# Half of the last 64 rows of wq read through GpSimd's queue, on one core of Trainium2: a decode step with a long key and value cache

## The chip, the cores and the metric

The kernel runs on one core of a Trainium2 chip. Its engines are TensorE (PE in the profile; PEld is its weight load), VectorE (DVE), ScalarE (ACT), GpSimd (POOL) and SyncE (SP). The metric is the time of one execution in device microseconds (us); lower is better. Comparisons below are of medians of several runs, and a profile is of one execution.

A DMA is issued by an engine's instruction and is carried out by the core's 16 DMA engines. In the profile the DMAs issued by SP are queue q1, those issued by ACT are q10, and q8 and q14 are fetches of instructions. "SPq", "ACTq" and "DVEq" stand for those engines' own sequencers. The trace also has a record for every DMA packet: its start, its duration, its size and its queue (which DMA engine carried it is not in the record).

## The reference

```python
def reference(A_x, A_k_cache, A_v_cache, A_wq, A_wo, B_x, B_w1, B_b1, B_w2, B_b2, gate_w):
    x = A_x                                        # (1, 1, 448), bf16
    g = _sigmoid((x * gate_w).sum(-1, keepdims=True))
    # a: 16 query heads over 8 key/value heads, 65536 cached positions, 256 per head
    q = (x @ wq).reshape(B, Sq, Hq, Dh).transpose(0, 2, 1, 3)
    scores = einsum("bhqd,bhkd->bhqk", q, repeat(k_cache, 2)) * Dh ** -0.5
    a = einsum("bhqk,bhkd->bhqd", softmax(scores), repeat(v_cache, 2)) ... @ wo
    # b: layernorm(x), then a small MLP over the sequence axis of length 1, 1792 wide
    b = gelu(layernorm(x) * w1 + b1) @ w2 + b2
    return g * a + (1 - g) * b
```

The two caches are 268 MB each; wq is 448 x 4096 (3.7 MB) and wo 4096 x 448 (3.7 MB). Everything else is small.

## The kernel before, in words

**Blocks.** The 65536 positions of each of the 8 key/value heads are cut into 4 blocks of 16384, so there are 32 blocks (L = 31 is the last). A block of keys or of values is 128 partitions x 64 KB, 8 MB, and is read by one DMA from SP's queue. Keys go to three half-block slots of `k_all`, values to `vt`. For each block DVE transposes keys (L395, eight times 128x2048), PE makes scores from them (L403, 64 matmuls), a running softmax follows (L460 to L504), and PE multiplies the probabilities with the values (L423). A loop (L581) runs 15 times over two blocks; the last two blocks are written out behind it (L615 to L680), where the values of block 31 come in eight pieces, the last two of 4 positions per partition each, and where wo's last piece is the last load.

**The head of the kernel.** Before the loop the kernel makes the queries and the small MLP. SP issues, in this order: the first 384 rows of wq (`wq_m`, L157: 128 partitions x 24 KB), the last 64 rows (`wq_t`, L158: each row in two halves, so that row r's halves are partitions 2r and 2r+1 with 4 KB each), then three loads of the keys of block 0 (L124: two of 2 MB and one of 4 MB). Both wq tiles lie in `vt`, so that the first load of values (L133) must wait until the queries are made. ACT issues x (`xr`), then the three small tables w1, b1 and w2 (L166; 14 rows of 256 bytes each, into `tables`), then `gw` and `b2b`.

POOL writes a constant (`ident`, by a memset and an affine select) and sets `qz` to zero (L206). DVE makes masks from `ident` (L176 to L188). Among them is `par`, which says to which of the two halves a partition of `wq_t` belongs. L217 doubles each of the last 64 values of x into `xrr`, in the order of the partitions of `wq_t`; a matmul turns it into a column (L226), and L234 multiplies it with `par` into `xtm`, the weights for `wq_t`.

The tables are transposed on PE (L248) and then read by DVE (L258, L259); DVE finishes the layernorm (L260 to L268), and ACT makes 14 gelu tiles (L273). PE makes the queries: for each of 32 columns three matmuls with `wq_m` (L284) and one with `wq_t` (L291). They are copied and spread by L299 to L317 (into `qz`). Then come memsets (L376 to L380), the gate's sum (L331, L332), ACT's `ez` (L333), and DVE's end of the MLP (L342 to L353), while PE sums the gelu tiles (L337). Then the loop is entered; all engines meet there, and SP issues the first load of values (L133).

**The order.** Each engine's instructions stand in the order of the program text (the helper `seq` ties each instruction to the one before it on its engine). The framework adds the waits; a DMA's completion semaphore is one of eight per kind of queue in turn, so that SP's second load of the head that takes a semaphore used before waits for the DMA that had it (L124's second load waits for `wq_m`).

Of the kernel before, what the change touches and what calls it, by code (L numbers as in the profile page):

```python
# [9 lines left out]
BF16 = mybir.dt.bfloat16  # L10
ACT = mybir.ActivationFunctionType
ALU = mybir.AluOpType
AXIS = mybir.AxisListType
# [4 lines left out]
REP = HQ // HKV  # L18
# [13 lines left out]
def kernel(  # L32
# [15 lines left out]
    nc = tc.nc  # L48

    D = A_x.shape[-1]  # L50
# [3 lines left out]
    NF = F // 128  # L54
# [6 lines left out]
    def seq(ins):  # L61
        e = ins.ins.engine
        if e in last:
            tc.add_manual_dep(
                ins.ins,
                last[e],
                mybir.DependencyInfo(
                    mybir.DependencyClass.NoSync, mybir.DependencyReason.DATA
                ),
                reason="program order",  # L70
            )
        last[e] = ins.ins.name
        return ins

    kvpool = ctx.enter_context(tc.tile_pool(name="kvpool", bufs=1))
    const = ctx.enter_context(tc.tile_pool(name="const", bufs=1))
# [24 lines left out]
    xr = const.tile([1, D], BF16)  # L101
    gw = const.tile([1, D], BF16)
    tables = const.tile([3 * NF, 128], BF16)
    w2b = const.tile([128, NF], BF16)
    b2b = const.tile([1, 1], BF16)
    DM = 384
    wq_m = vt[:, 0:48, :].rearrange("p a b -> p (a b)").rearrange("p (k n) -> p k n", k=3)
    wq_t = vt[:, 48:56, :].rearrange("p a b -> p (a b)")
# [40 lines left out]
    def load_v_last(n):  # L149
# [5 lines left out]

    seq(nc.scalar.dma_start(out=xr[:], in_=A_x[0, 0].rearrange("(o n) -> o n", o=1)))
    seq(nc.sync.dma_start(out=wq_m, in_=A_wq[0:DM, :].rearrange("(p k) n -> p k n", k=3)))  # L157
    seq(nc.sync.dma_start(  # L158
        out=wq_t[:, :], in_=A_wq[DM:D, :].rearrange("r (h n) -> (r h) n", h=2)
    ))  # L160
    for k, table in enumerate((
        B_w1[0].rearrange("(b p) -> b p", p=128),
        B_b1.rearrange("(b p) -> b p", p=128),
        B_w2.rearrange("(b p) o -> b (p o)", p=128),
    )):
        seq(nc.scalar.dma_start(out=tables[k * NF:(k + 1) * NF, :], in_=table))  # L166
    seq(nc.scalar.dma_start(out=gw[:], in_=gate_w.rearrange("(o n) -> o n", o=1)))
    seq(nc.scalar.dma_start(out=b2b[:], in_=B_b2.rearrange("(o n) -> o n", o=1)))
    load_k(0, 1, 1, ((0, 32), (32, KP)))
# [2 lines left out]

    ident = const.tile([128, 128], BF16)
    make_identity(nc, ident[:])
    ident_f = const.tile([128, 128], FP32)
    seq(nc.vector.tensor_copy(out=ident_f[:], in_=ident[:]))  # L176
    rowsel = ident_f[:].rearrange("p (a i r) -> p r a i", a=4, r=REP)
# [2 lines left out]
        out=val[:], in_=rowsel[:, :, :, 0:NI], op=ALU.add, axis=AXIS.XY  # L180
    ))
    fst = const.tile([128, 2, REP], FP32)
    for e in range(2):
        seq(nc.vector.tensor_reduce(
            out=fst[:, e, :], in_=rowsel[:, :, :, e:e + 1], op=ALU.add, axis=AXIS.XY
        ))
    par = const.tile([128, REP], FP32)
    seq(nc.vector.tensor_reduce(  # L188
        out=par[:], in_=ident_f[:].rearrange("p (a r) -> p r a", r=REP), op=ALU.add, axis=AXIS.X
    ))  # L190
    nval = const.tile([128, REP], FP32)
    seq(nc.vector.tensor_scalar(
        out=nval[:], in0=val[:], scalar1=-scale, scalar2=None, op0=ALU.mult
# [7 lines left out]
        out=same[:], in_=val[:].unsqueeze(1).to_broadcast([128, 64, REP])  # L201
# [7 lines left out]
        out=sel[:],  # L209
        in_=ident[:].rearrange("p (w k) -> p w k", w=NW).unsqueeze(2).to_broadcast([128, NW, NQ, 32]),  # L210
# [2 lines left out]

    xm = const.tile([128, 3], BF16)
    xtm = const.tile([128, REP], BF16)
    xrr = const.tile([1, D - DM, 2], BF16)
    seq(nc.vector.tensor_copy(  # L217
        out=xrr[:], in_=xr[:, DM:D].unsqueeze(2).to_broadcast([1, D - DM, 2])
    ))
    x_col = hd_ps[:, 40:44]  # L220
    for k in range(3):
        seq(nc.tensor.matmul(
# [1 line left out]
            rhs=ones_b[:, 0:1], start=True, stop=True,  # L224
        ))
    seq(nc.tensor.matmul(  # L226
        x_col[:, 3:4], lhsT=xrr[:].rearrange("o a r -> o (a r)"),
        rhs=ones_b[:, 0:1], start=True, stop=True,
    ))
    seq(nc.tensor.matmul(  # L230
# [4 lines left out]
        out=xtm[:], in0=par[:], scalar1=x_col[:, 3:4], scalar2=None, op0=ALU.mult  # L235
# [13 lines left out]
        t_ps, lhsT=tables[:, :], rhs=ident[0:3 * NF, 0:3 * NF], start=True, stop=True  # L249
# [5 lines left out]
        out=veps[:], in0=mv[:, 1:2], scalar1=1e-5, scalar2=None, op0=ALU.add  # L255
# [5 lines left out]
    for _ in range(2):  # L261
# [3 lines left out]
            out=ntmp[:], in0=ntmp[:], scalar1=-0.5, scalar2=1.5, op0=ALU.mult, op1=ALU.add  # L265
# [3 lines left out]
        out=h_bc, in0=xf, scalar1=mv[:, 0:1], scalar2=rstd[:, 0:1],  # L269
        op0=ALU.subtract, op1=ALU.mult,  # L270
    ))
    for b in range(NF):
        seq(nc.scalar.activation(  # L273
            out=gel[b], in_=h_bc, func=ACT.Gelu_apprx_tanh,
# [4 lines left out]
    for h in range(HQ):  # L279
        half, hh = divmod(h, HQ // 2)  # L280
        for c in range(2):
            col = c * HQ + h
            for k in range(3):
                seq(nc.tensor.matmul(  # L284
                    q_ps[:, col:col + 1],
                    lhsT=wq_m[:, k, h * DH:(h + 1) * DH].rearrange("p (d c) -> p c d", c=2)[:, c, :],
# [6 lines left out]
                lhsT=wq_t[:, hh * DH:(hh + 1) * DH].rearrange("p (d c) -> p c d", c=2)[:, c, :],  # L293
# [7 lines left out]
    for w in range(NW):  # L301
        seq(nc.tensor.matmul(
            qq_ps[:, w * 2 * HQ:(w + 1) * 2 * HQ],
            lhsT=sel[:, w, :, :].rearrange("p a k -> p (a k)"), rhs=qb[:],
# [3 lines left out]
    for k in range(2):  # L308
        seq(nc.vector.tensor_copy(
            out=qq[:, :, :, k, :], in_=qq_ps.rearrange("p (w g r) -> p w g r", g=HKV, r=REP)  # L310
# [304 lines left out]
    for n in (L - 1, L):  # L615
# [14 lines left out]
        else:  # L630
            def rest_base():
# [9 lines left out]
                out=lsv[:], in0=val[:], scalar1=lsum[:, 0:1], scalar2=None, op0=ALU.mult  # L641
# [8 lines left out]
                out=rdv[:], in0=rdv[:], scalar1=gcol[:, 0:1], scalar2=None, op0=ALU.mult  # L650
# [6 lines left out]
    for c in range(2):  # L657
        for e in range(2):
            seq(nc.tensor.matmul(
                o_last[:, c, :],  # L660
                lhsT=acc[:, e, :].rearrange("p (d c) -> p c d", c=2)[:, c, :],
# [5 lines left out]
        out=oT[:], in0=o_last, in1=rdv[:].unsqueeze(1).to_broadcast([128, 2, REP]), op=ALU.mult  # L667
# [43 lines left out]
```

## Time and profile before

| what | value |
|---|---|
| median of 3 runs | 1265.22 us (1265.11 to 1265.61) |
| the profiled execution's own time | 1265.1 us |
| its span in the profile | 1263.3 us |
| HBM read | 544.22 MB, 431 GB/s over the span |
| busy: PE, DVE, ACT, POOL | 805.5, 708.2, 59.5, 1.7 us |
| DMA packets | 13494 |

The span runs from the first instruction shown to the last; 1.8 us of the execution's own time lie outside it. Busy times say how long an engine worked, not what the kernel waits for. The DMA row of the profile gives, for 40 equal slices of the span, the mean busy share of the 16 DMA engines in tenths.

### The profile page before, as it was taken

The page shows a single profiled execution, that of the slowest core. Times are in us where ns is not written, and L with a number is a line of the kernel's source. Part 1 is how long each engine was busy: PE and PEld are TensorE (multiplying, and loading weights), DVE is VectorE, ACT ScalarE, POOL GpSimd, SP SyncE. Part 2 cuts the span into 40 slices and gives each one's busy share as a digit, 9 for nine tenths or more (in the row PEclk, how much of TensorE's full clock was granted, in tenths as well). Part 3 has the DMA queues.
Part 4 walks back from the last instruction along what each step waited for, and adds up shares of the span by engine and source line. Part 5 has one row for each costly group of instructions (what it writes and reads, how often), then busy time and mean ns, then how long its engine had stood idle before and what let it go on. Part 6 is the DMA issues. An engine that isn't in the chain of part 4 may idle for free.

```text
span 1263.3 us, 12073 instructions
## 1 busy us (share of the span) xinstructions
PE 805.5 (64%) x4690; PEld 319.1 (25%) x4690; DVE 708.2 (56%) x755; ACT 59.5 (5%) x132; POOL 1.7 (0%) x7
## 2 busy tenths in 40 slices
PE   4756567575576656666566766658666576665568
PEld 2222222222222222222222222213222232222224
DVE  4665456664556645566444665446654456654575
ACT  4000000000000000000000000000000000000000
POOL 0000000000000000000000000000000000000000
PEclk9977788777888777878778887788877787877879
DMA  9999999999999999999999999999999999999998
GB/s 414 430 439 432 433 438 432 433 438 433 432 438 433 432 435 436 426 440 436 429 438 422 442 438 422 442 424 438 440 424 436 435 432 436 435 432 439 427 437 343
DMA packets 13494, 544.36 MB, mean 431 GB/s; under 512 B 1577, under 2 KB 3628, under 8 KB 4140
## 3 DMA queue, kind: packets, MB, share of 16 engines
q1 hardware_dynamic: 13394, 544.22, 99.6%
q8 instruction: 6, 0.10, 0.0%
q10 hardware_dynamic: 90, 0.01, 0.0%
q14 instruction: 4, 0.03, 0.0%
HBM read 544.22 MB, written 0.00 MB: 431 GB/s over the span
## 4 chain that ended last, share of the span: by engine, by line
DMA 71%; PE 12%; DVE 12%; issue 4%; SPq 0%; DVEq 0%
DMA k_all<-in_A_k_cache_dram 67%; DVE kT L395 12%; PE sc L403 11%; DMA vt<-in_A_v_cache_dram 2%; DMA k_all<-in_A_v_cache_dram 2%; PE hd_ps L539 0%; SPq L130 0%; PE hd_ps L525 0%; PE f L672 0%; PE sm_ps L525 0%; DVEq L395 0%; DVE res L678 0%; PE hd_ps L448 0%; SPq L124 0%; DVE oT L666 0%
## 5 line engine op out<-in xcount | busy, mean ns | idle before, releaser
L403 PE MATMUL sc<-kT,qz 128*128 128x512 bf16 x2048 | 545.1, 416 | 322.1 <-DVE kT L395 321.8
L395 DVE STREAM_TRANSPOSE kT<-k_all 128x2048 f32<-128x2048 f32 x256 | 570.7, 2282 | 210.2 <-DMA k_all<-in_A_k_cache_dram 160.2
L403 PEld LDWEIGHTS <-qz 128*128 128x128 bf16 x2048 | 211.3, 103 | 658.2 <-issue 478.8
L423 PE MATMUL pv_ps<-vt,pT 128*4 128x512 bf16 x1968 | 175.2, 534 | 27.2 <-DVE pT L498 27.2
L504 DVE SCALAR_TENSOR_TENSOR acc<-acc,al,pv_ps 128x512 f32<-128x512 f32 x31 | 23.2, 747 | 163.6 <-PE pv_ps L423 163.6
L423 PEld LDWEIGHTS <-pT 128*4 128x4 bf16 x2000 | 58.0, 110 | 131.9 <-issue 88.0
L491 ACT ACTIVATE p_sb<-sc,nb 128x512 bf16<-128x512 f32 x32 | 22.0, 687 | 1031.5 <-DVE nb L487 1031.5
L460 DVE TENSOR_REDUCE rmax<-sc 128x1 f32<-128x512 f32 x32 | 22.1, 692 | 63.6 <-PE sc L403 63.6
L498 DVE STREAM_TRANSPOSE pT<-p_sb 128x512 bf16<-128x512 bf16 x32 | 22.8, 711 | 27.4 <-ACT p_sb L491 27.4
L510 PE MATMUL hd_ps<-lsum,same 128*128 128x1 f32 x30 | 7.6, 322 | 28.8 <-DVE lsum L499 28.8
L478 PE MATMUL sm_ps<-mrun,ones_f 1*128 1x2 f32 x64 | 12.1, 257 | 21.2 <-DVE mrun L477 13.0
L464 PE MATMUL sm_ps<-ident_f,rmax 128*1 128x128 f32 x32 | 8.7, 270 | 24.5 <-DVE rmax L460 24.5
L546 ACT COPY wo_sb<-wo_sb 128x896 bf16<-128x896 bf16 x16 | 15.0, 937 | 149.5 <-PE hd_ps L539 142.3
L525 PE MATMUL hd_ps<-esc,acc 128*128 128x2 f32 x60 | 9.9, 269 | 17.2 <-DVE acc L504 13.1
L539 PE MATMUL hd_ps<-wo_sb,oT 128*1 128x448 bf16 x60 | 20.8, 452 | 0.0
L543 DVE TENSOR_TENSOR a_acc<-a_acc,hd_ps 1x448 f32<-1x448 f32 x15 | 9.1, 608 | 17.4 <-PE hd_ps L539 17.4
L478 PEld LDWEIGHTS sm_ps<-mrun,ones_f 1*128 1x128 f32 x64 | 9.4, 183 | 27.4 <-DVE mrun L477 16.3
L525 PEld LDWEIGHTS hd_ps<-esc,acc 128*128 128x128 f32 x60 | 8.6, 204 | 25.4 <-DVE acc L504 20.2
L510 PEld LDWEIGHTS hd_ps<-lsum,same 128*128 128x128 f32 x30 | 6.3, 261 | 30.1 <-DVE lsum L499 30.1
L487 DVE CUSTOM_DVE_ANT_0 junk<-sm_ps,nval 128x2 f32<-128x2 f32 x32 | 5.1, 160 | 14.0 <-PE sm_ps L478 14.0
L464 PEld LDWEIGHTS sm_ps<-ident_f,rmax 128*1 128x1 f32 x32 | 2.5, 80 | 40.1 <-DVE rmax L460 40.1
L317 DVE COPY qz<-qq 32x16 bf16 (+1 forms) x64 | 10.5, 164 | 1.4
(117 smaller groups left out, 149.1 us busy)
## 6 DMA issues: line engine op xcount, KB each, us to landing
k_all<-in_A_k_cache_dram SPq DMA_DIRECT2D x3, 4096.0 KB
vt<-in_A_v_cache_dram SPq DMA_DIRECT2D x1, 5120.0 KB, 27.3
k_all<-in_A_k_cache_dram SPq DMA_DIRECT2D x2, 2048.0 KB
k_all<-in_A_v_cache_dram SPq DMA_DIRECT2D x2, 2048.0 KB
wo_sb<-in_A_wo_dram SPq DMA_DIRECT2D x16, 224.0 KB, 27.9
vt<-in_A_wq_dram SPq DMA_DIRECT2D x1, 3072.0 KB
vt<-in_A_v_cache_dram SPq DMA_DIRECT2D x1, 3072.0 KB
k_all<-in_A_v_cache_dram SPq DMA_DIRECT2D x3, 1024.0 KB
```

The costliest lines, as they stand in the source:

```text
L395: seq(nc.vector.transpose(out=kT_tiles[i % 2][:].rearrange("p j w k c -> p (j w k c)").bitcast(FP32), in_=slots[pair[i // 4]][:, i % 4 * N ...
L403: seq(nc.tensor.matmul(sc_tiles[e][:, :], lhsT=qz[:, 2 * w + c, 2 * (NI - i):2 * (NI - i) + 128], rhs=kT_tiles[i % 2][:, :, w, :, c], star ...
L423: seq(nc.tensor.matmul(dst[32 * grp:32 * grp + 2 * REP, :, :], lhsT=pT[:, 32 * jj + 2 * REP * ip:32 * jj + 2 * REP * (ip + 1)], rhs=pairs( ...
L460: seq(nc.vector.tensor_reduce(out=rmax[:], in_=sc_ps[:, :], op=ALU.max, axis=AXIS.X))
L478: seq(nc.tensor.matmul(sm_ps[:, 128:128 + REP], lhsT=ones_f[0:1, :], rhs=mrun[0:1, :], start=True, stop=True))
L491: seq(nc.scalar.activation(out=p_sb[:, :], in_=sc_ps[:, :], func=ACT.Exp, scale=scale, bias=nb[:, 0:1], accum_out=den[:, 0:1],))
L498: seq(nc.vector.transpose(out=pT[:, :], in_=p_sb[:, :]))
L504: seq(nc.vector.scalar_tensor_tensor(out=acc[:], in0=acc[:], scalar=al_tiles[e][:, 0:1], in1=src[:, :, :], op0=ALU.mult, op1=ALU.add,))
L510: seq(nc.tensor.matmul(hd_ps[:, 460:461], lhsT=same[:].rearrange("p a r -> p (a r)"), rhs=lsum[:, 0:1], start=True, stop=True,))
L525: seq(nc.tensor.matmul(o_ps[c], lhsT=acc[:, e, :].rearrange("p (d c) -> p c d", c=2)[:, c, :], rhs=weights[:, e, :], start=(start and e == ...
L539: seq(nc.tensor.matmul(a_ps, lhsT=oT[:, c, r:r + 1], rhs=wo_sb[:, r, c, :], start=(r == 0 and c == 0), stop=(r == REP - 1 and c == 1),))
L546: seq(nc.scalar.copy(out=wo_sb[:, 0], in_=wo_sb[:, 1]))
```

## The change

Four things are changed, all ahead of the loop. The 64 rows are now laid out by halves: partition r of `wq_t` in 64 to 127 holds the second half of row r, and partitions 0 to 63 hold first halves. The second halves stay on SP's queue (64 rows of 4 KB). The first halves are read by a DMA that POOL issues, whose source has 8 as its outermost dimension: row 8s + a goes to partition 8a + s. Ahead of it POOL issues a DMA of the first 8 rows of w1; ACT issues only rows 8 to 13 of it. DVE builds `xrr` with two copies in the place of one, in the new order of the rows, and `par` sums over the two halves of the partitions.

```diff
--- before.py
+++ after.py
@@ -155,15 +155,15 @@
 
     seq(nc.scalar.dma_start(out=xr[:], in_=A_x[0, 0].rearrange("(o n) -> o n", o=1)))
     seq(nc.sync.dma_start(out=wq_m, in_=A_wq[0:DM, :].rearrange("(p k) n -> p k n", k=3)))
-    seq(nc.sync.dma_start(
-        out=wq_t[:, :], in_=A_wq[DM:D, :].rearrange("r (h n) -> (r h) n", h=2)
-    ))
+    halves = A_wq[DM:D, :].rearrange("r (h n) -> h r n", h=2)
+    seq(nc.sync.dma_start(out=wq_t[64:128, :], in_=halves[1]))
+    w1_rows = B_w1[0].rearrange("(b p) -> b p", p=128)
+    seq(nc.scalar.dma_start(out=tables[8:NF, :], in_=w1_rows[8:NF, :]))
     for k, table in enumerate((
-        B_w1[0].rearrange("(b p) -> b p", p=128),
         B_b1.rearrange("(b p) -> b p", p=128),
         B_w2.rearrange("(b p) o -> b (p o)", p=128),
     )):
-        seq(nc.scalar.dma_start(out=tables[k * NF:(k + 1) * NF, :], in_=table))
+        seq(nc.scalar.dma_start(out=tables[(k + 1) * NF:(k + 2) * NF, :], in_=table))
     seq(nc.scalar.dma_start(out=gw[:], in_=gate_w.rearrange("(o n) -> o n", o=1)))
     seq(nc.scalar.dma_start(out=b2b[:], in_=B_b2.rearrange("(o n) -> o n", o=1)))
     load_k(0, 1, 1, ((0, 32), (32, KP)))
@@ -172,6 +172,10 @@
 
     ident = const.tile([128, 128], BF16)
     make_identity(nc, ident[:])
+    seq(nc.gpsimd.dma_start(out=tables[0:8, :], in_=w1_rows[0:8, :]))
+    seq(nc.gpsimd.dma_start(
+        out=wq_t[0:64, :], in_=halves[0].rearrange("(s a) n -> a s n", a=8)
+    ))
     ident_f = const.tile([128, 128], FP32)
     seq(nc.vector.tensor_copy(out=ident_f[:], in_=ident[:]))
     rowsel = ident_f[:].rearrange("p (a i r) -> p r a i", a=4, r=REP)
@@ -186,7 +190,7 @@
         ))
     par = const.tile([128, REP], FP32)
     seq(nc.vector.tensor_reduce(
-        out=par[:], in_=ident_f[:].rearrange("p (a r) -> p r a", r=REP), op=ALU.add, axis=AXIS.X
+        out=par[:], in_=ident_f[:].rearrange("p (h r) -> p h r", h=2), op=ALU.add, axis=AXIS.X
     ))
     nval = const.tile([128, REP], FP32)
     seq(nc.vector.tensor_scalar(
@@ -213,10 +217,12 @@
 
     xm = const.tile([128, 3], BF16)
     xtm = const.tile([128, REP], BF16)
-    xrr = const.tile([1, D - DM, 2], BF16)
+    xrr = const.tile([1, 2, D - DM], BF16)
     seq(nc.vector.tensor_copy(
-        out=xrr[:], in_=xr[:, DM:D].unsqueeze(2).to_broadcast([1, D - DM, 2])
-    ))
+        out=xrr[:, 0, :].rearrange("o (a s) -> o a s", a=8),
+        in_=xr[:, DM:D].rearrange("o (s a) -> o a s", a=8),
+    ))
+    seq(nc.vector.tensor_copy(out=xrr[:, 1, :], in_=xr[:, DM:D]))
     x_col = hd_ps[:, 40:44]
     for k in range(3):
         seq(nc.tensor.matmul(
@@ -224,7 +230,7 @@
             rhs=ones_b[:, 0:1], start=True, stop=True,
         ))
     seq(nc.tensor.matmul(
-        x_col[:, 3:4], lhsT=xrr[:].rearrange("o a r -> o (a r)"),
+        x_col[:, 3:4], lhsT=xrr[:].rearrange("o h r -> o (h r)"),
         rhs=ones_b[:, 0:1], start=True, stop=True,
     ))
     seq(nc.tensor.matmul(
```

On POOL the order before was: memset of `ident`, memset of `qz`, affine select. It is now: memset of `ident`, the DMA of 8 table rows, affine select, the DMA of 64 half rows, memset of `qz`. The matmul L248 now waits for one more DMA (the 8 table rows), the first matmul with `wq_t` (L291 before) for both halves' DMAs, and the loop's first load of values for both too. All lines behind the change move down by 4 to 6.

## The prediction

> **What bounds the kernel now.** I read the page's DMA rows first, then the timeline and the waits of both ends, then the trace's packet records.
>
> ```profile
> span 1263.3 us, 12073 instructions
> PE 805.5 (64%) x4690; PEld 319.1 (25%) x4690; DVE 708.2 (56%) x755; ACT 59.5 (5%) x132; POOL 1.7 (0%) x7
> ...
> DMA  9999999999999999999999999999999999999998
> ...
> q1 hardware_dynamic: 13394, 544.22, 99.6%
> q8 instruction: 6, 0.10, 0.0%
> ```
>
> No compute engine is above 64% while the DMA engines are at 9 in all slices but the last: the kernel streams 544.22 MB, and a stage's compute matters only if it leaves them without work. The packet records are sharper. From 2.0 to 1257 us all 16 engines always have a packet in hand; a 64-KB packet starts 2.414 us after the one before it on its engine, so the records link into 16 chains, one for each engine. They are equal in bytes and unequal in time. At the last piece of values the earliest chain is done at 1257.0, most by 1258.2, and one, which I call the slow engine, at 1258.81. It got behind by 0.3 us with its first packet (2.03 us, where the row for 24 KB is 0.912) and by 1.4 us when a 16-KB instruction packet (q8) fell on it at 50.7. Other late ones at that point: 1258.23 and 1258.11 (a q8 packet each, at 1215 and 1248) and 1258.16.
>
> Two chains lead to the end, both through the slow engine. These are the timeline's rows (start, duration, engine, line, work, idle before and its releaser):
>
> ```profile
> 1200.92 4.50 DVE L395 STREAM_TRANSPOSE kT<-k_all 128x2048 f32<-128x2048 f32 x2 [6.34 <-DMA k_all<-in_A_k_cache_dram]
> ...
> 1259.20 0.35 PE L448 MATMUL hd_ps<-pT,k_all 128*128 128x2 bf16 x8 [0.16 <-DMA k_all<-in_A_v_cache_dram]
> ```
>
> DVE starts on block 30's keys after waiting 6.34 us for them: the slow engine's share ended at 1200.46, the next one's at 1199.53. From there DVE and PE run nearly without a gap, and at the end PE waits 0.16 us for the last values, again the slow engine's. Both move one for one with the slow engine; if only one moves, the other stops the gain after 0.16 us, or at once.
>
> So a change in the head counts in one of two ways: it empties the DMA queues, or it shifts work among the 16 engines. The rows for the first, the head's timeline:
>
> ```profile
> 11.78 0.19 DVE L258 COPY wb<-hd_ps 128x28 f32<-128x28 f32 x1 [4.44 <-PE hd_ps L248]
> ...
> 23.49 1.28 ACT L333 ACT_TABLE_LOAD   x1
> ...
> 25.02 0.14 DVE L342 TENSOR_SCALAR gate<-ez 1x1 f32<-1x1 f32 x1 [4.04 <-ACT ez L333]
> ...
> 28.09 0.35 SPq L133 DMA_DIRECT2D vt<-in_A_v_cache_dram  x1
> ```
>
> DVE idles 4.44 us for the tables and 4.04 us for ACT. The first load of values is issued at 28.09; from issue to first packet the first load took 1.03 us (0.74 to 1.77), so it is ready at 29.1, while the engines end block 0's keys between 30.37 and 31.37. That is a cover of 1.3 us, and of 2.0 us or more for the late engines.
>
> **The change part by part.**
>
> Bytes: none added or removed. At 431 GB/s nothing is won by the split as such.
>
> The spread over engines. In the trace a table of 14 rows puts one 256-byte packet on each of 14 chains and none on two, 128 rows put eight packets on each of 16, one row goes to one. Rows are dealt out by the outermost dimension. So 8 outermost should mean eight engines with eight rows each, and SP's 64 rows sixteen with four each. A 4-KB packet takes 0.159 us, 0.155 from start to start. Before, each engine had 8; after, eight engines have 12 and eight have 4. That is +0.62 us on one half of the engines and -0.62 on the other, and since no engine idles afterwards, it stays to the end. The 8 + 6 table rows move 18-ns packets, 0.04 us at most.
>
> [...] No row here shows a GpSimd DMA.
>
> Is the slow engine on the relieved half? The records have no engine numbers. The table rows ahead take eight engines first; if engines are dealt in turn, the half rows get the other eight, so I take the relieved half to be the low one (a choice, no row shows it) and rank the chains by their first packet: the engine that alone has `xr` and `gw` (number 0) is second at 1.790, the two without tables (14, 15) are 11th and 13th. The slow engine is third, at 1.792, so it is probably low. The late chains at 1258.16 (fourth) and 1258.11 (ninth) are low and doubtful; the one at 1258.23 started late (2.627) and can't be placed. With the slow engine relieved it ends at 1258.19. If a late chain is on the loaded half, it ends at 1258.73 to 1258.85 and becomes the new last: the gain is then between 0.08 and nothing. If none is, it is 0.62. The compute chain gains up to 0.62 either way. I take the middle, -0.3 us.
>
> POOL. No row shows a DMA issued by it. The nearest rows are SP's and ACT's issues, 0.33 to 0.53 us; the upper bound is the whole of the 4.44 us that DVE idles before L258. I take the 1.06 us of the memset that each issue stands beside. The affine select came at 1.97, behind that memset; now it is behind one issue, so it stays near 2.0. Everything that hangs on `ident` (L176 to L254, ended at 7.34) is hidden by DVE's wait for the tables; with that cover gone each us late would be a us in L258. Zeroing `qz` moves behind two issues, to about 4 us; its reader L317 starts at 16.86. One more `xrr` copy: 0.20 us by L217's row (bounds 0.1 and 0.4), under the same cover; `par` keeps its 128 inputs. No gain below nothing, as DVE waits for the tables anyway.
>
> The tables (ACT's queue). Small and large packets alternate on an engine: on one chain the table packets start at 5.36, 6.28, 7.20, 8.12, each behind a 0.912 us packet. The last w2 row landed at 11.30. Six engines keep three rows, eight have two, and POOL's own rows need two turns of their own. I cost it at nothing; bounds: -1.8 us (two turns) and +0.8 (five 4-KB packets in between), and neither reaches the DMA queues (cover 1.3 us).
>
> The half rows. They must land before the first `wq_t` matmul (12.37; the old load landed at 12.33). With one packet a turn, from 5.4 on as ACT's queue had: 11 packets (table row, its semaphore, eight rows, semaphore) are five turns while 24-KB packets run (to 10.9), four of 0.32 beside SP's 4-KB rows, two of 0.77 beside 16-KB keys: 13.7, landed about 14.2, 1.9 us later. Queued behind that wait on PE are the queries and the sum L337; on DVE L299 to L332, whose last result is ready at 20.98 and is needed when ACT's table load ends at 24.77. So 3.8 us of cover: nothing. The large first part of wq shares its engine with up to eight of these packets, +1.2 us, and SP's second load of keys waits for it:
>
> ```profile
> SPq L124 <- DMA vt<-in_A_wq_dram: 8.7, 1, 8.7
> ```
>
> It would be issued at about 12.3 in place of 11.1, while the keys issued earlier last to 15.8. Nothing.
>
> Sum: -0.3 us. The profiled execution took 1265.1, of which 1.8 lie outside the span; it is 0.1 below the median of the runs. So 1265.2 - 0.3 = **1264.9 us**.
>
> **The rivals.**
> - *The slow engine is on the loaded half.* For: nothing fixes which half is relieved. Against: the order of the first packets. Both end chains get +0.62: 1265.8.
> - *No shift.* The rows are dealt over all 16 engines, or a different engine is slow in each execution (first packets took 0.91 to 2.52 us): 1265.2. [...]
> - *The half rows land late (the slower side).* L291's place on PE holds the queries, these `ez`, that the loop. It costs nothing until they land at 16.1 (12.33 + 3.8), then eats the 2.0 us of queued keys, and from 18.1 on each us late is a us. If POOL's queue gets only every second turn, 6.5 packets are left at 12.2 and take 13 turns of 0.77: landed near 22.7, 4.6 us lost: 1269.8. Against: the tables' regular turns on ACT's queue.
> - *Something outside the span* (a queue more to set up and drain) cannot be seen in a trace without one; from nothing to a few us.
>
> **How the numbers follow.** Relief 0.50 (1264.5 to 1265.2), loaded half 0.26, no shift 0.12, late rows 0.06, outside the span 0.04, a gain that I don't see 0.02. Relief, loaded half and no shift make 0.88, between 1264.5 and 1265.8; with 0.3 for runs differing, and a margin above for a small cost outside the span, the range is 1264.2 to 1266.8. 0.2% is 2.5 us, about what a measurement of this kernel tells from no change; the first three cases, and half of the fourth and fifth, lie within it. Faster 0.02, same 0.91, slower 0.07.
>
> **What the profile after would show.** A queue with 64 packets of 4 KB and 8 of 256 bytes; eight chains with twelve 4-KB packets and eight with four; the late chains' ends moved by 0.6 us, up or down; DVE's start on block 30's keys moved like the slow engine; L133 still near 28 us. What would make it wrong: an L133 after 30 us, a DMA slice under 9 at the start, or 4-KB packets spread evenly.

## The result and the profile after

The changed kernel takes 1267.62 us (median of 20 runs, 1267.21 to 1268.43), the kernel before 1265.01 us beside it (20 runs, 1264.33 to 1265.61). The ratio is 1.0021 with a 95% interval of 1.0015 to 1.0028: slower by 2.6 us. The forecast was 1264.9, in a range that ended at 1266.8. The profiled execution took 1267.44 us with a span of 1265.7, so 1.74 us lie outside the span (1.8 before): all of the loss is inside it.

The page of the changed kernel, the lines that answer to those shown of before, with the row of rates added:

```profile
span 1265.7 us, 12079 instructions
PE 801.1 (63%) x4690; PEld 318.4 (25%) x4690; DVE 709.9 (56%) x756; ACT 59.6 (5%) x132; POOL 3.0 (0%) x9
...
DMA  9999999999999999999999999999999999999998
GB/s 373 437 436 433 436 433 431 438 431 436 433 431 438 431 438 431 431 438 431 438 431 437 432 435 434 431 438 431 435 434 435 434 433 439 428 437 432 429 438 340
...
q1 hardware_dynamic: 13330, 543.96, 99.5%
q0 software_dynamic: 176, 0.26, 0.1%
q8 instruction: 6, 0.10, 0.0%
```

The new queue q0 is GpSimd's. DVE works 1.7 us longer (1.4 of it one cast in the head, see the last section) and POOL 1.3; the DMA row still has a 9 in its first slice. By the packet records no DMA engine ran dry: from 3 to 1240 us all sixteen always have a packet in hand. But the rate of that first slice is 373 GB/s, where the kernel before has 414, the first number of its row:

```profile
GB/s 414 430 439 432 433 438 432 433 438 433 432 438 433 432 435 436 426 440 436 429 438 422 442 438 422 442 424 438 440 424 436 435 432 436 435 432 439 427 437 343
```

Engines with slow packets count as busy here (a 9 at 373 GB/s), so the loss shows in the rates and not in the busy shares.

Where in the slice? Busy time by stretches of 2 us from 8 to 16 (the last two columns are the DMA share and GB/s; packets are not cut at the edges, so single rows swing), first before, then after:

```profile
8.00:10.00 2.00, 0.00 (x0) 0.00 (x0) 0.00 (x0) 0.88 (x1) 0.00 (x0) 1.00 0.90 382
10.00:12.00 2.00, 0.19 (x1) 0.20 (x2) 0.22 (x3) 0.00 (x0) 0.00 (x0) 1.00 1.11 461
12.00:14.00 2.00, 1.84 (x63) 1.75 (x63) 1.69 (x11) 0.00 (x0) 0.00 (x0) 1.00 0.99 426
14.00:16.00 2.00, 1.87 (x71) 1.81 (x68) 0.30 (x2) 1.76 (x3) 0.00 (x0) 1.00 1.01 434
```

```profile
8.00:10.00 2.00, 0.00 (x0) 0.00 (x0) 0.88 (x3) 1.00 (x2) 0.00 (x0) 1.00 1.17 427
10.00:12.00 2.00, 0.00 (x0) 0.00 (x0) 0.00 (x0) 0.49 (x1) 0.00 (x0) 1.00 0.84 194
12.00:14.00 2.00, 0.41 (x4) 0.34 (x4) 1.28 (x9) 0.00 (x0) 0.00 (x0) 1.00 1.14 272
14.00:16.00 2.00, 0.86 (x32) 0.87 (x33) 0.83 (x3) 1.05 (x2) 0.00 (x0) 1.00 0.92 385
```

The mean over the four rows falls from 426 to 320 GB/s while the share stays near 1. 106 GB/s missing for 8 us are 0.85 MB, at 431 GB/s 2.0 us. The packet records say the same, and say which packets are slow: all that are in flight then. A 16-KB packet of keys takes up to 1.40 us (0.611 before), a 4-KB half row up to 0.47 on SP's queue and 0.33 on GpSimd's (0.159), a 24-KB row up to 1.28 (0.912). All sixteen 24-KB rows that start from 9.09 us on take 1.10 or more, though only half of the chains carry any of GpSimd's half rows. The excess over the durations in brackets, summed and divided by 16 engines, is 2.05 us. Nothing gives it back: the first large piece of keys ends on average at 18.32 (16.14 before, +2.2), block 30's keys on average 2.2 us later, on the last engine 2.4 us later. Counted in bytes moved, at 431 GB/s, the changed kernel is 2.2 us behind the kernel before at 16 us, and still 2.1 behind at 1200.

The end of the kernel (columns as before: start, duration, engine, line, work, idle before it and its releaser), changed kernel:

```profile
1203.28 4.51 DVE L401 STREAM_TRANSPOSE kT<-k_all 128x2048 f32<-128x2048 f32 x2 [5.72 <-DMA k_all<-in_A_k_cache_dram]
...
1259.22 2.71 PE L454 MATMUL hd_ps<-pT,k_all 128*128 128x2 bf16 x96
```

DVE starts on block 30's keys 2.36 us later than before (1200.92), and the span is 2.4 longer. At the end PE runs its 96 last matmuls without waiting for a DMA; before, it waited 0.16 us ahead of the last 8. So the chain through DVE alone carries the loss to the end.

### The profile page after: what moved, and what is told of

Its sections match the earlier page's. It is cut to its first block, busy times and chain, and to the rows that moved or that the text cites. A ratio compares the mean times of both kernels' runs of the same rounds, so it can differ in the third digit from the quotient of the medians.

```text
span 1265.7 us, 12079 instructions
## 1 busy us (share of the span) xinstructions
PE 801.1 (63%) x4690; PEld 318.4 (25%) x4690; DVE 709.9 (56%) x756; ACT 59.6 (5%) x132; POOL 3.0 (0%) x9
## 4 chain that ended last, share of the span: by engine, by line
DMA 67%; PE 14%; DVE 12%; issue 4%; SPq 0%; ACT 0%; DVEq 0%; ACTq 0%
DMA k_all<-in_A_k_cache_dram 67%; PE sc L409 13%; DVE kT L401 12%; PE hd_ps L454 0%; PE pv_last L429 0%; PE hd_ps L545 0%; SPq L130 0%; DVE rmax L466 0%; PE hd_ps L665 0%; ACT p_sb L497 0%; PE hd_ps L531 0%; PE pv_ps L429 0%; PE sm_ps L531 0%; PE sm_ps L484 0%; DVE pT L504 0%
## 5 line engine op out<-in xcount | busy, mean ns | idle before, releaser
L429 PE MATMUL pv_ps<-vt,pT 128*4 128x512 bf16 x1968 | 170.6, 522 | 27.3 <-DVE pT L504 27.3
```

The costliest lines, as they stand in the source:

```text
L429: seq(nc.tensor.matmul(dst[32 * grp:32 * grp + 2 * REP, :, :], lhsT=pT[:, 32 * jj + 2 * REP * ip:32 * jj + 2 * REP * (ip + 1)], rhs=pairs( ...
```

## The experiments

Four theories could explain slow packets in this stretch. **A**: the reads; each DMA now reads every second 4 KB of HBM, not whole rows. **B**: GpSimd's queue slows whatever runs beside it. **C**: the destination; each load now writes 64 partitions, not 128. **D**: a load through eight engines is slow. The first four kernels separate them. The kernel before beside them had 1264.77 us.

### The half rows in natural order (against D)

GpSimd's load has 64 as its outermost dimension, in place of 8. In the trace its rows lie on all 16 chains. (The copies into `xrr` follow; that part of the edit isn't shown.)

```diff
-        out=wq_t[0:64, :], in_=halves[0].rearrange("(s a) n -> a s n", a=8)
+        out=wq_t[0:64, :], in_=halves[0]
```

> The changed kernel, but POOL's DMA reads its 64 half rows in their natural order (64 outermost, so up to 16 engines with four rows each in place of eight with eight); the table rows stay on POOL. In the changed kernel all DMA engines fall to about 225 GB/s in total between 9 and 14 us (16-KB key packets take up to 1.4 us in place of 0.611), which makes up the 2.2 us by which every later load is late. Theory A (addresses: a load that reads only one 4-KB half of every 8-KB row slows all reads): the dip stays, 1267 to 1268 us. Theory B (a GpSimd queue that carries 4-KB rows slows all engines): the dip stays, 1267 to 1268. [...] Theory D (eight engines with the rows of all): the dip goes, 1265.0 to 1265.5.

Measured: 1266.89 us (1266.56 to 1267.58), ratio 1.0017 (1.0007 to 1.0026). Most of the loss stays, and so does the dip (table below), as by A, B and C, for which I had expected 1267 to 1268. The outermost 8 is not what costs.

### Both halves on SP's queue (against B)

```diff
+    seq(nc.sync.dma_start(out=wq_t[0:64, :], in_=halves[0]))
     seq(nc.sync.dma_start(out=wq_t[64:128, :], in_=halves[1]))
-    seq(nc.gpsimd.dma_start(out=tables[0:8, :], in_=w1_rows[0:8, :]))
-    seq(nc.gpsimd.dma_start(
-        out=wq_t[0:64, :], in_=halves[0].rearrange("(s a) n -> a s n", a=8)
-    ))
```

ACT reads all table rows again, as before, and the copies into `xrr` follow (neither is shown).

> Both halves as two 64-row DMAs on SP's queue, all table rows on ACT's, nothing on POOL's queue; the layout of wq_t by halves stays. A (addresses): the dip stays, as each DMA still reads one 4-KB half of every row; 1266 to 1268 us. B (GpSimd's queue): no dip, 1265.0 to 1265.5. C (64 partitions on 16 engines): dip, 1266 to 1268. D (eight engines): no dip, 1265.0 to 1265.5.

Measured: 1266.96 us (1266.42 to 1267.94), ratio 1.0016 (1.0007 to 1.0026), without any DMA of GpSimd's. The dip stays and 4-KB packets take up to 0.48. One side effect spoils the size: SP has one load more, so that the first load of keys takes the semaphore of `wq_m` and is issued only at 11.67. From 11.5 to 13.6 us some engines have no packet, so that the 106 GB/s near 12 us are partly an empty queue; the 269 at 10 us are not.

### Whole rows as the source (against A)

```diff
-    halves = A_wq[DM:D, :].rearrange("r (h n) -> h r n", h=2)
+    halves = A_wq[DM:D, :].rearrange("(g r) (h n) -> g (r h) n", g=2, h=2)
```

Each DMA reads 32 whole rows, one unbroken stretch of 256 KB; queues and destinations are those of the change. The queries are then made with these weights in another order.

> The changed kernel, queues, engines and destinations kept, but each of the two DMAs reads 32 whole rows, an unbroken 256 KB, in place of one half of 64 rows. The queries are then made with the weights of the last 64 rows in another order, so the output differs. A (addresses): no dip, 1265.0 to 1265.8 us. B (GpSimd's queue): dip, 1267 to 1268. C (64 partitions on 16 engines): dip, 1267 to 1268. D (eight engines): dip, 1267 to 1268.

Measured: 1267.39 us (1267.24 to 1270.28), ratio 1.0023 (1.0013 to 1.0034), the dip unchanged. A falls.

### The load of before, issued by GpSimd (B and C)

```diff
-    seq(nc.sync.dma_start(
-        out=wq_t[:, :], in_=A_wq[DM:D, :].rearrange("r (h n) -> (r h) n", h=2)
-    ))
...
     make_identity(nc, ident[:])
+    seq(nc.gpsimd.dma_start(
+        out=wq_t[:, :], in_=A_wq[DM:D, :].rearrange("r (h n) -> (r h) n", h=2)
+    ))
```

> The kernel before, but the whole load of wq's last 64 rows (128 partitions, unbroken 512 KB, in the layout of before) is issued by POOL in place of SP, at the changed kernel's place; the tables stay on ACT. A (addresses): no dip, 1265.0 to 1265.8 us. B (GpSimd's queue): dip, 1267 or more, as twice the rows come this way. C (64 partitions on 16 engines): no dip, 1265.0 to 1265.8. D (eight engines): no dip, 1265.0 to 1265.8.

Measured: 1266.03 us (1265.34 to 1267.76), ratio 1.0011 (1.0002 to 1.0021). No dip at all: every 4-KB packet takes 0.159 us. B falls as the cause of the dip. But 1.3 us are lost, 0.2 more than the range allowed, and elsewhere, which I had not foreseen. The first packets of values take up to 3.2 us (2.42 in steady state), and the rate from 30 to 34 us is 401, 380, 390, 407 (428, 419, 423, 426 before). In bytes moved this stretch costs 0.3 us in the trace; another 0.5 goes between 100 and 500 us, a little at a time. The loop is entered later, too:

```profile
28.80 0.35 SPq L133 DMA_DIRECT2D vt<-in_A_v_cache_dram  x1
```

(28.09 before.) C is left. The second four kernels test it by itself, in a sharper form, **C1** ("shared shares" in the last four): it depends on which partitions a load writes. I assumed that a load to all 128 or to 32 to 95 keeps the rate, and that one to 0 to 63 or to 64 to 127 brings it to half. Which partitions an engine writes is not in the records. The kernel before beside them had 1264.82 us. Loads called extra bring 256 KB that nobody reads, 0.6 us at 431 GB/s.

### An extra load to partitions 32 to 95, and one to 64 to 127 (C1)

The kernel before, with SP's extra load behind the keys of block 0. The two differ in two numbers:

```diff
     load_k(0, 0, 0)
+    spare = early[:, 12288:14336]
+    seq(nc.sync.dma_start(
+        out=spare[32:96, :], in_=A_wq[DM:D, :].rearrange("r (h n) -> h r n", h=2)[1]
+    ))
```

> The kernel before, plus one more DMA on SP's queue behind the keys of block 0: 64 rows of 4 KB (half rows of wq, as in the change) into an unused stretch of the third key slot, partitions 32 to 95, read by nobody. 256 KB more are 4 packets of 0.155 us on each engine, +0.6 us if nothing else happens. [...] Theory C2 (any 64-row load, four rows for an engine, is slow): a dip, packets near 0.3, 1266.0 or more.

> The same extra 64 rows at the same place in the queue, into partitions 64 to 127, as SP's half in the changed kernel. [...] C2: the same as with partitions 32 to 95.

Measured: 1265.72 us (1265.5 to 1266.45) with 32 to 95 and 1266.94 us (1266.68 to 1267.4) with 64 to 127; ratios 1.0005 (0.9996 to 1.0014) and 1.0015 (1.0006 to 1.0024). Both lie in what I expected by C1 (1265.2 to 1265.8 and 1266.0 to 1267.0). The ranges of the runs don't touch: the partitions alone are worth 1.22 us. In the records the median 4-KB packet takes 0.159 us in the one, with 90% at or under that, and 0.228 in the other, with 10% over 0.392; the 64-KB packets beside those take up to 3.9 us (3.1 in the one). This is C1, on SP's queue, without the change. But there is a dip with 32 to 95 too, though I had expected none near 31 us: from 31 to 32 us, where the first packets of values follow, the rate is 297 GB/s, and 243 with 64 to 127 (419 before). In bytes moved, from 30 to 36 us, the one loses 0.5 us and the other 1.4. (The execution profiled for 32 to 95 took 1266.45 us, the longest of its eleven.)

### An extra load through eight engines (C1 and D)

The kernel before, with GpSimd reading 64 extra half rows, 8 outermost, to partitions 0 to 63.

```diff
     make_identity(nc, ident[:])
+    spare = early[:, 12288:14336]
+    seq(nc.gpsimd.dma_start(
+        out=spare[0:64, :],
+        in_=A_wq[DM:D, :].rearrange("r (h n) -> h r n", h=2)[0].rearrange("(s a) n -> a s n", a=8),
+    ))
```

> The kernel before, plus one more DMA issued by POOL at the changed kernel's place: 64 half rows with 8 outermost into an unused stretch of the third key slot, partitions 0 to 63, read by nobody. It is the POOL part of the change alone, without SP's 64-row load. 256 KB are +0.6 us on average, +1.2 on eight engines. [...] C2 (four rows for an engine is what is slow): no dip, 1265.4 to 1266.2.

Measured: 1267.55 us (1267.31 to 1268.25), ratio 1.0021 (1.0012 to 1.003), 0.55 above the 1266.0 to 1267.0 that I expected by C1. The dip is there, 4-KB packets up to 0.37. The first large piece of keys ends 1.96 us later than before, 1.35 more than the extra bytes take.

### The rows cut by columns (C1)

All 128 partitions in both loads: GpSimd reads the first 2 KB of each half row, SP the other 2 KB.

```diff
-    seq(nc.sync.dma_start(
-        out=wq_t[:, :], in_=A_wq[DM:D, :].rearrange("r (h n) -> (r h) n", h=2)
-    ))
+    tail = A_wq[DM:D, :].rearrange("r (h n) -> (r h) n", h=2)
+    seq(nc.sync.dma_start(out=wq_t[:, 1024:2048], in_=tail[:, 1024:2048]))
...
     make_identity(nc, ident[:])
+    seq(nc.gpsimd.dma_start(out=wq_t[:, 0:1024], in_=tail[:, 0:1024]))
```

> The layout of before with its 128 partitions, but each 4-KB row is cut in two: POOL's queue reads the first 2 KB of all 128 partitions, SP's queue the second 2 KB. As in the change half of the bytes come through POOL, but each DMA is spread over all 128 partitions. C1: no dip, 2-KB packets at 0.084; 1264.8 to 1265.8. C2: eight rows for an engine, no dip, the same. If a dip comes, both fall and GpSimd's queue is back in question (though the whole load through it showed none).

Measured: 1266.33 us (1265.88 to 1267.54), ratio 1.0012 (1.0003 to 1.0021). The same bytes on the same two queues, and next to no dip. But 1.5 us remain, 0.5 more than the range for C1 allowed, as with the load that GpSimd issued whole: slow first packets of values, up to 3.3 us.

### Without GpSimd's table rows

The last four kernels ran beside 1264.90 us of the kernel before.

```diff
-    seq(nc.scalar.dma_start(out=tables[8:NF, :], in_=w1_rows[8:NF, :]))
+    seq(nc.scalar.dma_start(out=tables[0:NF, :], in_=w1_rows[0:NF, :]))
...
-    seq(nc.gpsimd.dma_start(out=tables[0:8, :], in_=w1_rows[0:8, :]))
```

> The changed kernel without GpSimd's table rows: ACT reads all 14 rows of w1 again, and the half rows are GpSimd's only DMA. [...] Rival, the table rows matter: if they set which engines carry the half rows, or hold them up, the dip gets smaller by a third or more and the time comes under 1266.9. Whether the eight engines are the ones that carry three or two of ACT's table rows is read from the packets; no time hangs on it.

Measured: 1268.11 us (1267.67 to 1268.56), ratio 1.0024 (1.0015 to 1.0033), 0.3 above the 1267.2 to 1267.8 that I expected by C1. The dip starts about 2 us earlier (the rate falls under 400 GB/s at 7 us, in the changed kernel at 9), since the half rows are now GpSimd's first DMA, and is as deep. The table rows are not the cause; they held the half rows back.

### The change on other partitions

The decisive one: the change with queues, table rows, 8 outermost and bytes kept, and other partitions. SP's half rows go to 32 to 95, GpSimd's in two DMAs of 32 rows to 0 to 31 and 96 to 127; `par` and `xrr` follow (not shown). One thing more differs: in the trace GpSimd's second DMA of half rows runs on the other eight chains, so that its rows lie on all 16, four each, where the changed kernel has eight each on eight. The kernel with the natural order had them on all 16 too and kept its dip.

```diff
-    seq(nc.sync.dma_start(out=wq_t[64:128, :], in_=halves[1]))
+    seq(nc.sync.dma_start(out=wq_t[32:96, :], in_=halves[1]))
...
-    seq(nc.gpsimd.dma_start(
-        out=wq_t[0:64, :], in_=halves[0].rearrange("(s a) n -> a s n", a=8)
-    ))
+    for lo, p in ((0, 0), (32, 96)):
+        seq(nc.gpsimd.dma_start(
+            out=wq_t[p:p + 32, :],
+            in_=halves[0][lo:lo + 32].rearrange("(s a) n -> a s n", a=8),
+        ))
```

> [...] Shared shares: SP's part of the loss (about 1.2 us, as between the two kernels with extra loads) goes. [...] Rival, any load cut into 64 rows or through eight engines costs this, wherever it lands: 1267.4 or more, with the same dip.

Measured: 1266.37 us (1266.18 to 1267.84), ratio 1.0012 (1.0003 to 1.0021); 1.74 below the kernel just above, and 1.25 below the changed kernel, which was measured apart from it. I had expected 1265.6 to 1266.4 if GpSimd's part of the loss went with SP's, 1266.4 to 1266.9 if it stayed in part. The same stretches as for the two kernels at the start:

```profile
8.00:10.00 2.00, 0.00 (x0) 0.00 (x0) 0.48 (x3) 1.40 (x2) 0.00 (x0) 1.00 1.00 426
10.00:12.00 2.00, 0.31 (x4) 0.32 (x4) 0.40 (x4) 0.09 (x1) 0.00 (x0) 1.00 1.06 431
12.00:14.00 2.00, 1.21 (x45) 1.15 (x44) 1.72 (x9) 0.00 (x0) 0.00 (x0) 1.00 0.98 418
14.00:16.00 2.00, 2.00 (x81) 2.00 (x79) 0.00 (x0) 1.97 (x4) 0.00 (x0) 1.00 1.01 434
```

The dip is gone: 427 GB/s on average, all 128 half rows at 0.159 us, all 16-KB packets at 0.611. The first large piece of keys ends on average at 16.25, 0.1 us after that of before. So the dip and its 2.2 us go with the partitions that the two loads write. But only 1.25 to 1.74 us of the time come back, since part is lost again at the loop's entry, as in the two kernels whose GpSimd loads covered all partitions. In bytes moved this kernel is 0.1 us behind the kernel before at 16 us and 0.9 from 36 us on; the changed kernel is 2.2 behind at both.

```profile
28.39 0.35 SPq L133 DMA_DIRECT2D vt<-in_A_v_cache_dram  x1
...
1201.82 4.50 DVE L409 STREAM_TRANSPOSE kT<-k_all 128x2048 f32<-128x2048 f32 x2 [5.17 <-DMA k_all<-in_A_k_cache_dram]
```

Block 30's keys are used 0.9 us later than before. The first packets of values take up to 4.0 us; their excess over 2.418 adds up to 10.2 us, 0.64 for each engine. And from 30.5 to 31.8 us up to six engines have no packet in hand, 0.21 us for each engine on average.

### GpSimd's extra load to 32 to 95, and to 0 to 63

The kernel before, with GpSimd reading 64 extra half rows in natural order; the two differ in the partitions.

```diff
     make_identity(nc, ident[:])
+    spare = early[:, 12288:14336]
+    seq(nc.gpsimd.dma_start(
+        out=spare[32:96, :], in_=A_wq[DM:D, :].rearrange("r (h n) -> h r n", h=2)[0]
+    ))
```

> The kernel before with 64 half rows (256 KB) read once more by GpSimd, in natural order, to partitions 32 to 95 of an unused part of the tile; nobody reads them. [...] Rival, GpSimd's loads are slow on their own whatever their partitions: 1267.3 or more, as the one with eight outermost had.

> As the one before, but to partitions 0 to 63. [...] Rival, the partitions don't matter for GpSimd's loads: within 0.4 us of the one before.

Measured: 1266.73 us (1265.75 to 1267.19) and 1267.19 us (1266.57 to 1269.69), ratios 1.0012 (1.0003 to 1.0021) and 1.0021 (1.0011 to 1.0032). By C1 I had expected 1265.7 to 1266.7 and near 1267.5. The medians differ by 0.46, less than the 1.0 to 1.5 that I expected, and the runs overlap: by time alone this pair is inconclusive. In the traces, of executions of 1265.88 and 1267.09 us, the keys' first large piece ends 0.95 us apart (17.14 and 18.09), in the direction of C1. I had expected no dip for 32 to 95, and there is a shallow one, to 381 GB/s.

### All rates side by side

GB/s in bins of 1 us, from the packet records, each packet spread over its duration:

```
from us                            8   9  10  11  12  13  14  15
before                           431 427 420 427 432 432 432 431
after                            420 367 325 220 232 235 334 430
half rows in natural order       358 309 302 260 227 252 369 431
both halves on SP's queue        431 425 269 225 106 234 400 429
whole rows as the source         424 370 292 207 233 258 354 430
before's load, by GpSimd         429 429 425 429 429 430 432 431
extra, eight engines, 0-63       358 354 365 350 269 359 428 432
cut by columns                   417 404 411 420 431 432 432 431
without table rows               339 343 336 264 257 220 235 394
other partitions                 429 428 416 420 431 432 432 431
GpSimd's extra, 32-95            419 390 381 388 426 432 431 431
GpSimd's extra, 0-63             324 312 323 337 405 427 432 432
```

All kernels with a load to 0 to 63 or 64 to 127 in this stretch fall below 325; none of the others falls below 380. At the bottom of the changed kernel's dip, 220 to 235 GB/s, the rate is about half of 431.

## Why the prediction was wrong

**The step that failed** is the first of the sum: "Bytes: none added or removed. At 431 GB/s nothing is won by the split as such", together with the price of a half row in the next, 0.155 us wherever it lands. Both took the 431 GB/s as a property of the 16 engines that a split cannot touch. In these runs it held, or nearly (381 GB/s at the lowest between 8 and 16 us), only where no load in that stretch went to 0 to 63 or to 64 to 127. The row that I priced by, 4 KB in 0.159 us, came from a load to all 128 partitions, and I did not ask what a load to 64 would make of it. Missing term: +2.2 us (2.0 from the rates, 2.05 from the packets, 2.2 from the keys' landing).

**The shift between engines** (-0.62 on one half, +0.62 on the other) was the whole of my sum. It is there, underneath the loss: the ends of the first large piece of keys form two groups of eight, with means of 17.84 and 18.81 us, 0.97 apart (1.24 forecast). The other kernels with GpSimd's rows on eight engines have 0.90 to 1.24 between the earlier and the later eight, the one with the natural order 0.50, the kernel before 0.36. But the loss lies on all engines, and the last engine, 0.93 us behind the next one at block 30's keys before, is 0.12 behind it now.

The half was chosen wrongly, too. The forecast let the engines be dealt in turn, so that the table rows ahead would send the half rows to another eight. No run shows that rule, on which the choice of the half in its -0.3 us rests, and in the changed kernel the half rows went to the same eight: in the trace the eight chains with a 256-byte q0 packet are those on which q0's 4-KB packets follow, from 7.4 us on. The two chains without any table row of ACT's, 14 and 15 by the forecast's count, are not among them. So the loaded half was the low one, which I had taken to be relieved; by my own sum that was the rival with 1265.8. In the change on other partitions a third DMA did go to the other eight. When GpSimd's DMAs change over is not shown.

**The rivals.** "No shift", with 1265.2, let the split change nothing. The shift is there (0.97 us between the two groups), and the split cost 2.6 us. The slower rival priced late half rows, the wrong mechanism: they were late as forecast and did not matter.

**What held.** The head of the changed kernel:

```profile
1.31 0.66 POOL L175 DMA_DIRECT2D tables<-in_B_w_dram  x1 [0.36 <-issue]
2.28 0.62 POOL L176 DMA_DIRECT2D vt<-in_A_wq_dram  x1
2.39 1.66 DVE L180 CAST ident_f<-ident 128x128 f32<-128x128 bf16 x1 [2.39 <-POOL ident masks.py:199]
2.86 1.11 POOL L210 MEMSET qz<- 128x1152 bf16 x1
...
12.49 0.19 DVE L264 COPY wb<-hd_ps 128x28 f32<-128x28 f32 x1 [3.54 <-PE hd_ps L254]
...
15.13 0.19 PE L297 MATMUL hd_ps<-xtm,vt 128*128 128x1 bf16 x1 [2.10 <-DMA vt<-in_A_wq_dram]
...
25.73 0.14 DVE L348 TENSOR_SCALAR gate<-ez 1x1 f32<-1x1 f32 x1 [1.99 <-ACT ez L339]
...
29.25 0.36 SPq L133 DMA_DIRECT2D vt<-in_A_v_cache_dram  x1
```

- POOL's issues take 0.66 and 0.62 us (1.06 taken), and DVE's wait for the tables still covers them, with 3.54 us of 4.44 left.
- The tables come 0.7 us later (the copy at 12.49, before 11.78), near the upper bound of +0.8 and not at nothing. ACT's `ez` and so the entry into the loop move by as much.
- The first matmul with `wq_t` starts at 15.13, where landing near 14.2 was forecast. The cover of DVE's wait for `ez` was 4.04 us and is 1.99: late rows cost nothing, as forecast.
- L133 was to stay near 28, with 30 as the sign of being wrong, and is at 29.25: 0.7 from the tables, and 0.5 from DVE's last instruction to the issue (1.18 us, 0.72 before; DVE's end is `rest`, at 28.07 and 27.37). The engines end block 0's keys only from 32.15 on, so values are in the queue in time. (Before, the last engine ended them at 31.86, not at 31.37 as I had read; the first one, on which the cover rests, stands.)
- SP's second load of keys waited for `wq_m`, 8.7 us before; 9.9 was forecast (8.7 + 1.2), and 9.9 it is. That is luck. I had put up to eight half rows ahead of the end of `wq_m`; in the trace two lie ahead of a chain's last 24-KB row, and the rest is the dip, in which that row takes up to 1.28 us. In the change on other partitions, where two lie ahead as well, the wait is 8.6 us.

```profile
SPq L124 <- DMA vt<-in_A_wq_dram: 9.9, 1, 9.9
```

- Outside the span nothing changed (1.74 us, 1.8 before).

**What stays open.** (1) Two loads to half of the partitions would lose 0.6 us each if only their own 256 KB moved at half rate; each loses about twice that (1.22 us in SP's extra load, 1.35 in the one through eight engines, 2.2 for the two of the change). Packets of the other engines are slowed too, by which rule no run shows. (2) The 1.3 to 1.5 us that remain where GpSimd's loads cover all partitions: the whole load, the columns, the other partitions. In the traces the loss at the loop's entry, from 30 to 36 us, is 0.3, 1.05 and 0.8 us in bytes moved, and nothing in the changed kernel. Part of it is engines without a packet, 0.07, 0.45 and 0.21 us for each engine (0.01 before): the cover of 1.3 us that the forecast gave the first load of values was not there, though L133 came at most 0.8 us later than before. The rest is slow first packets of values. Their excess does not follow the time from L133 to the first engine's end of keys: 1.5 us for the whole load by GpSimd (excess 4.7 us in sum), 2.1 for the change on other partitions (10.2), 1.6 for GpSimd's extra load to 0 to 63 (2.0). SP's extra load to 32 to 95 has it too (3.0 us), without GpSimd. In the changed kernel it is absent (0.2). What makes them slow is not shown. (3) The shallow dip of GpSimd's extra load to 32 to 95, where C1 has none.

## What to carry to other kernels

Before a load is split, ask which partitions each part writes: here, with the queues full, parts that cover 0 to 63 and 64 to 127 brought the rate of everything in flight down to half (220 to 235 GB/s of 431), and a kernel that the transfers bound never got the time back (2.1 us behind at 1200 us). Cutting by columns (404 GB/s at the lowest), or writing 32 to 95 in one part and 0 to 31 with 96 to 127 in the other (416), took the dip away. It did not make the split worth while: both such kernels still took 1.5 us more than the load in one piece. The 0.159 us of a 4-KB packet was its price at that destination and beside those neighbours: in the changed kernel it is up to 0.47. And look for such a loss in the rates and in the durations of packets of one size, since the busy share of the DMA engines stayed at 9 here while the first slice had 373 GB/s in place of 414.

## What the runs showed of the hardware

- DVE's cast of `ident` (L176 before, 0.23 us) takes 1.66 us in the changed kernel and 1.05 where GpSimd issued the whole load. In both it ends 0.08 us after POOL's memset of `qz`, which used to be done before it started. In the change on other partitions the cast stands beside GpSimd's DMA issues alone and takes 0.23 us again:

```profile
2.27 1.12 POOL L177 DMA_DIRECT2D vt<-in_A_wq_dram  x2
2.38 0.23 DVE L182 CAST ident_f<-ident 128x128 f32<-128x128 bf16 x1 [2.38 <-POOL ident masks.py:199]
```

  So these issues alone did not hold the cast. There it is the two DVE instructions beside the memset that are held, 0.16 and 0.15 us long in the kernel before:

```profile
3.18 1.30 DVE L202 TENSOR_SCALAR nval<-val 128x2 f32<-128x2 f32 x1
3.36 1.10 POOL L216 MEMSET qz<- 128x1152 bf16 x1
3.53 1.08 DVE L210 COPY same<-val 128x128 f32<-128x128 f32 x1
```

  What holds them beside the memset is not shown. In the changed kernel the cast starts 0.47 us ahead of the memset, and is held all the same.
- GpSimd's two DMAs in the changed kernel also leave packets on engines that carry none of their rows: 104 of q0's 176 packets have 4 bytes, 11 on each of the eight chains without rows.
